# Gate, up and most of down products as 64-row couples on both halves of the array, with new load order and row grouping

## The chip, the cores and the metric

The kernel runs on one core of a Trainium2 chip. The metric is the device time of one execution in microseconds; "span" is the time from the first to the last instruction in the profile of one execution, some 2 us shorter than the time of the same execution.

Engines are named as in the profile: PE does the matrix products (PEld loads their weights), DVE the vector work, ACT the activations, POOL the third elementwise engine, SP issues transfers.

## The reference, cut to what matters

One transformer-like layer over 2048 tokens of width 448: layer norm, linear attention with 16 heads of 28 and a softmax feature map, a residual, layer norm, a gated feed-forward of width 1792, a residual.

```python
def _A_ref(x, wqkv, w_phi, wo):                    # x is already normalised
    q, k, v = split(x @ wqkv)                      # 448 x 1344
    pq = einsum("bhsd,hdf->bhsf", q, w_phi)
    pk = einsum("bhsd,hdf->bhsf", k, w_phi)
    phi_q = concatenate([softmax(pq), softmax(-pq)], axis=-1)
    phi_k = concatenate([softmax(pk), softmax(-pk)], axis=-1)
    kv = einsum("bhsf,bhsd->bhfd", phi_k, v)       # needs every token before any output
    z  = einsum("bhsf->bhf", phi_k)
    ...                                            # num / den, then @ wo

def _B_ref(x, w_gate, w_up, w_down):
    h = sigmoid(x @ w_gate) * (x @ w_up)           # 448 x 1792 each
    return h @ w_down                              # 1792 x 448

h  = x + _A_ref(layernorm(x), wqkv, w_phi, wo)
h2 = h + _B_ref(layernorm(h), w_gate, w_up, w_down)
```

Two facts matter. `kv` sums over all 16 tiles of 128 tokens, so no output of attention exists before the last tile's k features: that is the front of the kernel. And the contraction of gate and up, 448, is three and a half times 128: the array has 128 rows, so each gate and each up product has a remainder of 64 rows.

## The kernel before

The kernel is a graph of named operations. Each engine runs its operations in a fixed, hand-kept order (a list of names per engine), and semaphores are derived from reads and writes of tiles and PSUM banks. The feed-forward works in blocks of 128 of the 1792 columns, two blocks at a time ("a pair of blocks"). Before the change, a pair of blocks was three full gate products, three full up products, a couple of 64-row products for the remainders (gate on rows 0 to 63 of the array, up on rows 64 to 127, side by side), then the same with the couple first:

```python
def full(e, w, b, st, sp):
    for kt in range(3):
        p = e.matmul(bk(b)[:, 0:N], lhsT=w[:, kt, fs], rhs=hb[:, kt, ns],
                     start=(st and kt == 0), stop=(sp and kt == 2))
    return p

def pair(e, st):
    e.matmul(bk(bg)[:, 0:N], lhsT=wg_sb[0:64, 3, fs], rhs=hb[0:64, 3, ns], start=st, stop=not st)
    return e.matmul(bk(bu)[:, 0:N], lhsT=wu_sb[64:P, 3, fs], rhs=hb[64:P, 3, ns], start=st, stop=not st,
                    tile_position=(64, 0))
# even block: full(gate), full(up), pair    odd block: pair, full(gate) | full(up)
```

Down was 14 full products for each token tile. The loads of the front are made with k and v weights in separate transfers and one token tile's 128 rows spread one to a partition.

```python
x_t   = A_x[0].rearrange("(n p) d -> p n d", p=P)
out_t = out[0].rearrange("(n p) d -> p n d", p=P)
...
xload(0, 1, 100)
...
xload(1, 2, 97)
wload(1, "wk", 96.5)
wload(2, "wv", 96)
xload(2, 4, 95)
...
def warm(n):                       # products of zeros, to have the clock released early
    def f(e):
        for _ in range(n):
            p = e.matmul(bk(7)[:, 0:512], lhsT=zero[:, 0:P], rhs=zero[:], start=True, stop=True)
        return p
    return f
op("pe", "warm", warm(10), r=["zero"], w=[B(7)], dur=10 * 0.43, prio=100)
```

The k weights are transposed on PE, evicted, multiplied with `w_phi` (one product fewer per token later), evicted, and only then does the first k product run.

The softmax here doesn't subtract the row's maximum and nothing guards it: scores larger than these inputs give would overflow.

## Time and profile before

The time before is 224.34 us (median of four runs, 222.31 to 225.28). The span of the profiled execution, 222.8 us, falls into parts:

| part of the span | from, to (us) | length |
|---|---|---|
| start to first exp of k | 0, 12.80 | 12.80 |
| first exp of k to first gate product | 12.80, 71.14 | 58.34 |
| first gate product to start of the last product | 71.14, 219.30 | 148.16 |
| start of the last product to the end | 219.30, 222.8 | 3.5 |

PE's timeline: start, length of the group, engine, line, operation, tiles, shapes, count, and in brackets the idle time before it with what ended it.

```profile
1.49 3.62 PE L405 MATMUL psum<-zero 128*128 128x512 bf16 x10 [1.49 <-DVE zero L373]
6.14 0.62 PE L424 MATMUL psum<-ident,wqkv_sb 112*112 112x112 bf16 x8 [1.03 <-DMA wqkv_sb<-in_A_wqkv_dram]
...
9.69 0.92 PE L526 MATMUL psum<-wqkv_sb,xnT 112*128 112x448 bf16 x4
11.02 0.92 PE L526 MATMUL psum<-Wk,xnT 112*128 112x448 bf16 x4 [0.41 <-ACT Wk L445]
```

The k weights are in use at 6.14, released by their transfer, and the first k product starts at 11.02; the exponential of its result starts at 12.80. Four products in 0.92 us (their starts 0.19 apart) are at full speed.

The trace also holds records of the clock that was granted to PE. Here it was released at 4.13 us, during the warm-ups, and fell back to half speed from 24.61 to 28.03 us: the 7 in the row of the granted clock on the page.

In the second part ACT was the most loaded elementwise engine (windows view: length, then busy us and count of PE, PEld, DVE, ACT, POOL, granted clock, transfer share, GB/s):

```profile
12.80:71.14 58.34, 53.97 (x431) 33.80 (x428) 44.60 (x105) 52.52 (x107) 40.37 (x50) 0.97 0.68 145
```

### The profile page before, as it was taken

How to read it: one execution, taken by the hardware profiler on the slowest of the kernel's cores; microseconds unless marked ns; L12 is line 12 of the kernel's file. 1: busy time of each engine (PE TensorE's matmuls, PEld its weight loads, DVE VectorE, ACT ScalarE, POOL GpSimd, SP SyncE). 2: the span in 40 equal slices, each digit the busy share in tenths (PEclk: the TensorE clock that was granted, in tenths of full speed). 3: DMA queues.
4: the chain of work that ended last, by engine and by line, in shares of the span. 5: the costliest groups of instructions: out<-in, count | busy, mean ns of one | idle time of the engine just before them, and what ended most of it. 6: DMA issues, size and time to landing. Idle time of an engine off the chain costs nothing.

```text
span 222.8 us, 3721 instructions
## 1 busy us (share of the span) xinstructions
PE 210.5 (94%) x1392; PEld 111.4 (50%) x1402; DVE 137.9 (62%) x340; ACT 105.4 (47%) x219; POOL 67.4 (30%) x112
## 2 busy tenths in 40 slices
PE   6677899999998999999999999999999999999994
PEld 2444466666655666667634434433444344544351
DVE  3776977874978996799788858253531344232342
ACT  2797799987999554312343453233310322022210
POOL 5579789882344422222331410110000000000000
PEclk9999799999999999999999999999999999999999
DMA  6669899954004234204123131100010000010011
GB/s 156 153 170 147 210 167 272 218 164 128 0 0 74 47 71 57 42 24 91 27 49 71 30 66 47 24 14 9 24 41 0 22 24 21 0 41 21 3 41 41
DMA packets 31530, 15.61 MB, mean 70 GB/s; under 512 B 22936, under 2 KB 30616, under 8 KB 31512
## 3 DMA queue, kind: packets, MB, share of 16 engines
q1 hardware_dynamic: 31008, 15.34, 31.7%
q8 instruction: 11, 0.18, 0.3%
q10 hardware_dynamic: 504, 0.03, 0.2%
q14 instruction: 7, 0.06, 0.1%
HBM read 8.28 MB, written 1.84 MB: 45 GB/s over the span
## 4 chain that ended last, share of the span: by engine, by line
PE 80%; ACT 10%; DMA 6%; issue 1%; POOL 1%; DVE 0%; SPq 0%
PE psum L739 34%; PE psum L777 19%; PE psum L744 7%; PE psum L526 6%; PE psum L690 5%; PE psum L561 4%; PE psum L654 3%; ACT xn_pad L507 3%; DMA wqkv_sb<-in_A_wqkv_dram 2%; DMA xnT<-xn_pad 2%; PE psum L553 2%; DMA oT<-o_pad 2%; ACT hhT L537 1%; ACT hhT L536 1%; ACT WkT L429 1%
## 5 line engine op out<-in xcount | busy, mean ns | idle before, releaser
L764 ACT ACTIVATE sg_sb<-psum 128x512 bf16<-128x512 f32 (+1 forms) x70 | 35.7, 509 | 88.4 <-PE psum L745 80.8
L767 DVE TENSOR_TENSOR hhT<-psum,sg_sb 128x512 bf16<-128x512 f32 (+1 forms) x70 | 40.3, 581 | 45.2 <-ACT sg_sb L764 35.8
L739 PE MATMUL psum<-xnT,wu_sb 128*128 128x512 bf16 (+1 forms) x207 | 47.3, 336 | 0.3
L739 PE MATMUL psum<-xnT,wg_sb 128*128 128x512 bf16 (+1 forms) x203 | 46.7, 337 | 0.3 <-issue 0.2
L777 PE MATMUL psum<-wd_sb,hhT 128*128 128x448 bf16 x224 | 46.0, 352 | 0.1
L777 PEld LDWEIGHTS psum<-wd_sb,hhT 128*128 128x128 bf16 x224 | 21.8, 98 | 19.9 <-DVE hhT L767 0.2
L739 PEld LDWEIGHTS psum<-xnT,wu_sb 128*128 128x128 bf16 x210 | 20.5, 98 | 15.9
L739 PEld LDWEIGHTS psum<-xnT,wg_sb 128*128 128x128 bf16 x210 | 17.3, 97 | 22.1 <-issue 11.9
L545 POOL TENSOR_TENSOR phi<-hhT,rs 128x896 bf16<-128x896 bf16 x16 | 26.9, 1698 | 4.3 <-DVE rs L543 3.4
L676 POOL TENSOR_TENSOR o_pad<-c_sb,rden 128x448 bf16<-128x448 bf16 x16 | 14.9, 936 | 29.0 <-DVE rden L674 28.8
L541 DVE TENSOR_REDUCE ss<-hhT 128x32 f32<-128x896 bf16 x16 | 17.1, 1070 | 5.3 <-ACT hhT L537 5.2
L783 DVE TENSOR_TENSOR x_sb<-psum,x_sb 128x448 bf16<-128x448 f32 x16 | 9.9, 624 | 15.5 <-PE psum L777 15.0
L745 PE MATMUL psum<-xnT,wu_sb 64*128 64x512 bf16 (+1 forms) x70 | 18.1, 338 | 0.0
L744 PE MATMUL psum<-xnT,wg_sb 64*128 64x512 bf16 (+1 forms) x70 | 18.1, 338 | 0.0
L526 PE MATMUL psum<-Wk,xnT 112*128 112x448 bf16 x64 | 15.2, 363 | 2.8 <-DMA xnT<-xn_pad 2.3
L526 PE MATMUL psum<-wqkv_sb,xnT 112*128 112x448 bf16 x64 | 15.2, 368 | 1.2 <-ACT v L539 1.2
L561 PE MATMUL psum<-xnT,Wq 112*112 112x512 bf16 x64 | 16.2, 382 | 0.0
L690 PE MATMUL psum<-wo_sb,oT 112*128 112x448 bf16 x64 | 14.7, 352 | 0.3 <-DMA oT<-o_pad 0.3
L701 POOL TENSOR_SCALAR ve<-ssq 128x1 f32<-128x1 f32 x16 | 3.0, 190 | 39.0 <-ACT junk L698 38.8
L698 ACT ACTIVATE junk<-x_sb,nm 128x448 bf16<-128x448 bf16 x16 | 10.7, 671 | 7.7 <-DVE nm L696 7.6
L477 DVE BATCH_NORM_STATS2 st<-x_sb 128x6 f32<-128x448 bf16 x16 | 9.4, 612 | 5.5 <-DMA x_sb<-in_A_x_dram 5.5
L693 DVE SCALAR_TENSOR_TENSOR x_sb<-psum,x_sb 128x448 bf16<-128x448 f32 x16 | 9.9, 617 | 2.6 <-PE psum L690 2.3
(80 smaller groups left out, 249.7 us busy)
## 6 DMA issues: line engine op xcount, KB each, us to landing
out_dram<-x_sb SPq DMA_DIRECT2D x16, 112.0 KB, 1.7
wd_sb<-in_B_w_down_dram SPq DMA_DIRECT2D x7, 224.0 KB, 3.0
wu_sb<-in_B_w_up_dram SPq DMA_DIRECT2D x3, 448.0 KB, 4.5
wg_sb<-in_B_w_gate_dram SPq DMA_DIRECT2D x3, 448.0 KB, 4.0
wqkv_sb<-in_A_wqkv_dram SPq DMA_DIRECT2D x3, 392.0 KB, 4.8
x_sb<-in_A_x_dram SPq DMA_DIRECT2D x2, 448.0 KB, 4.5
x_sb<-in_A_x_dram SPq DMA_DIRECT2D x3, 224.0 KB, 4.3
wo_sb<-in_A_wo_dram SPq DMA_DIRECT2D x1, 392.0 KB, 3.7
```

The lines of the kernel that those rows point to most:

```text
L526: p = e.matmul(bk(bank)[:, 0:D], lhsT=xnT[t // 4][:GP, kt, TS(t)], rhs=wap(kt), start=(kt == 0), stop=(kt == KT - 1))
L541: op("dve", "ss%d" % t, lambda e: e.tensor_reduce(ss[:, s, :], ek[:, s, :, :].rearrange("p a (h d) -> p (a h) d", d=DH), AX.X, ALU.add), r ...
L545: op("pool", "phi%d" % t, lambda e: e.tensor_tensor(phi[:, sp, :, :].rearrange("p a (h d) -> p (a h) d", d=DH), ek[:, s, :, :].rearrange(" ...
L561: p = e.matmul(bk(b)[:GP, 0:512], lhsT=W2[1][:, kt, gg * GP:(gg + 1) * GP], rhs=xnT[c][:GP, kt, :], start=(kt == 0), stop=(kt == KT - 1))
L676: op("pool", "o%d" % t, lambda e: e.tensor_tensor(o_pad[:, s, :, 0:GP].rearrange("p g (h d) -> p g h d", h=4), c_sb[:, s, :, 0:DH].rearran ...
L690: p = e.matmul(bk(2)[:, 0:D], lhsT=oT[:GP, s, kt, :], rhs=wo_sb[:, kt, :], start=(kt == 0), stop=(kt == KT - 1))
L739: p = e.matmul(bk(b)[:, 0:N], lhsT=w[:, kt, fs], rhs=hb[:, kt, ns], start=(st and kt == 0), stop=(sp and kt == 2))
L744: e.matmul(bk(bg)[:, 0:N], lhsT=wg_sb[0:64, 3, fs], rhs=hb[0:64, 3, ns], start=st, stop=not st)
L745: return e.matmul(bk(bu)[:, 0:N], lhsT=wu_sb[64:P, 3, fs], rhs=hb[64:P, 3, ns], start=st, stop=not st, tile_position=(64, 0))
L764: op("act", "sig%d_%d" % (ci, ff), lambda e: e.activation(sg_sb[:, k, 0:N], bk(bg)[:, 0:N], ACT.Sigmoid), r=[B(bg), "sigtab"], w=[("sg", k ...
L767: op("dve", "hh%d_%d" % (ci, ff), lambda e: e.tensor_tensor(hhT[(t0 // 4) % NHH][:, ff, ns], bk(bu)[:, 0:N], sg_sb[:, k, 0:N], ALU.mult), ...
L777: p = e.matmul(bk(b)[:, 0:D], lhsT=hhT[c % NHH][:, ff, TS(t)], rhs=wd_sb[:, ff, :], start=(ff == 0), stop=(ff == FT - 1))
```

## The change

Its intent is to stop PE from switching between full products and 64-row products in the feed-forward: gate and up use 64-row couples throughout (low half of the array for one, high half for the other), the last three groups of token tiles do down the same way, and each pair of blocks or tiles swaps which bank each half writes to midway, so that each output gets all its rows. Beside that the change reorders the loads, loads k and v weights together in two halves of rows, gives each partition 16 consecutive token rows, moves thirteen operations (four evictions of k weights, five of v, three of transposed tokens and a normalisation) from ACT to DVE, against, on balance, two more evictions of q weights on ACT, and regenerates every engine's order. It also cuts the preparation of the k weights differently: each transposition needs only one of the two row halves, and each product with `w_phi` only one eviction in place of four. The core of the diff:

```diff
-    x_t = A_x[0].rearrange("(n p) d -> p n d", p=P)
-    out_t = out[0].rearrange("(n p) d -> p n d", p=P)
+    x_t = A_x[0].rearrange("(p n) d -> p n d", p=P)
+    out_t = out[0].rearrange("(p n) d -> p n d", p=P)
...
-        wload(1, "wk", 96.5)
-        wload(2, "wv", 96)
+        wload(0, 2, 1, 3, [("wkv", 0), ("wkv", 1)], "ld_kv0", 99, 220.0)
+        wload(2, 4, 1, 3, [("wkv", 2), ("wkv", 3)], "ld_kv1", 97, 220.0)
...   # order of SP: which transfers are asked for first
-        "x0 ld_wk x1 x2 ld_wv x4 x6 x8 ld_wq xT4 x12 ..."
+        "x0 x1 x2 x4 ld_kv0 ld_kv1 x8 x10 xT4 xT5 ld_q ..."
...
+        def both(e, lo, hi):
+            for a in range(max(len(lo), len(hi))):
+                for l, row in ((lo, 0), (hi, 64)):
+                    if a < len(l):
+                        o, w, r, st, sp = l[a]
+                        p = e.matmul(o, lhsT=w, rhs=r, start=st, stop=sp, tile_position=(row, 0))
+            return p
...
+            def f1(e):     # four couples: gate low, up high
+                return both(e, [(og, wg_sb[LO, kt, fs], hb[LO, kt, ns], kt == 0, False) for kt in range(4)],
+                            [(ou, wu_sb[HI, kt, fs], hb[HI, kt, ns], kt == 0, False) for kt in range(4)])
+            def f2(e):     # three couples, banks swapped
+                return both(e, [(ou, wu_sb[LO, kt, fs], hb[LO, kt, ns], False, kt == 2) for kt in range(3)],
+                            [(og, wg_sb[HI, kt, fs], hb[HI, kt, ns], False, kt == 2) for kt in range(3)])
...   # order of PE, one pair of blocks (even f1, odd f1, even f2, odd f2)
-        "gu0_0 gg0_1 uu0_1"
+        "ga0_0 ga0_1 gb0_0 gb0_1"
...   # a PE operation waits on PE itself when a bank changes halves
+            if o.eng == "pe":
+                return self.crosses(p, o)
...   # down of tiles 4 to 15, two tiles at a time, swapped midway
+                    def part(i, s):
+                        return [(bk(b[i])[:, 0:D], hb[s, ff, TS(t + i)], wd_sb[s, ff, :], ph == 0 and ff == 0,
+                                 ph == 1 and ff == FT - 1) for ff in range(a, a + n)]
+                    return both(e, part(i, LO), part(j, HI))
```

## The prediction

> **What bounds the kernel now.** I read the page first (busy shares, the row of slices, the granted clock), then the windows view over three stretches, then the PE waits of the first stretch, then the timeline of PE inside the late stage and of all engines in the tail.
>
> ```profile
> PE 210.5 (94%) x1392; PEld 111.4 (50%) x1402; DVE 137.9 (62%) x340; ACT 105.4 (47%) x219; POOL 67.4 (30%) x112
> ...
> PE   6677899999998999999999999999999999999994
> ...
> PEclk9999799999999999999999999999999999999999
> ```
>
> PE is loaded from end to end, but the first five slices (5.6 us each) are at 6 to 8 tenths, and the fifth ran at a lower clock. I split the span at the first v product (9.7), the first gate product (71.1) and the last stretch of down products (213).
>
> ```profile
> 9.70:71.10 61.40, 56.62 (x447) 35.14 (x446) 46.88 (x109) 55.58 (x113) 42.79 (x58) 0.97 0.66 142
> 71.10:213.00 141.90, 141.26 (x868) 69.61 (x876) 83.05 (x211) 45.62 (x100) 20.03 (x39) 1.00 0.16 35
> 213.00:222.80 9.80, 6.64 (x36) 3.23 (x33) 3.13 (x5) 0.00 (x0) 0.00 (x0) 0.99 0.14 47
> ```
>
> Columns: length, then busy us of PE, PEld, DVE, ACT, POOL. In the first stretch ACT (55.6 of 61.4) is as loaded as PE (56.6), so PE waits for it in part. In the second PE is never idle (141.3 of 141.9): only shorter PE work shortens it. PE's waits between 9 and 72 us:
>
> ```profile
> PE psum L526 <- DMA xnT<-xn_pad: 2.3, 1, 2.3
> PE psum L526 <- ACT v L539: 1.2, 1, 1.2
> ```
>
> "Busy" hides slower steps, so I looked at starts in the late stage. This is one pair of feed-forward blocks (gate and up of two blocks), between two runs of down products:
>
> ```profile
> 183.64 2.06 PE L777 MATMUL psum<-wd_sb,hhT 128*128 128x448 bf16 x10
> 185.53 0.81 PE L739 MATMUL psum<-xnT,wg_sb 128*128 128x512 bf16 x3
> 186.18 0.81 PE L739 MATMUL psum<-xnT,wu_sb 128*128 128x512 bf16 x3
> 186.92 0.39 PE L744 MATMUL psum<-xnT,wg_sb 64*128 64x512 bf16 x1
> 186.92 0.39 PE L745 MATMUL psum<-xnT,wu_sb 64*128 64x512 bf16 x1
> 187.15 0.38 PE L744 MATMUL psum<-xnT,wg_sb 64*128 64x512 bf16 x1
> 187.15 0.38 PE L745 MATMUL psum<-xnT,wu_sb 64*128 64x512 bf16 x1
> 187.46 0.82 PE L739 MATMUL psum<-xnT,wg_sb 128*128 128x512 bf16 x3
> 188.12 0.81 PE L739 MATMUL psum<-xnT,wu_sb 128*128 128x512 bf16 x3
> 188.76 1.49 PE L777 MATMUL psum<-wd_sb,hhT 128*128 128x448 bf16 x7
> ```
>
> Ten down products of 448 columns start over 1.89 us: 0.189 each, so 0.216 for 512 columns. The pair of blocks has 14 such slots (12 full products and two 64-row couples, each couple one slot, its halves starting together): 14 x 0.216 = 3.02. It takes 188.76 - 185.53 = 3.23. The missing 0.21 lies at the two borders between full and 64-row products: 186.18 to 186.92 is 0.74 where 0.65 is due, 187.15 to 187.46 is 0.31 where 0.22 is due. One change of mode costs 0.105 us. There are 35 such pairs (five groups of token tiles, seven pairs each) and so 70 changes, 7.3 us. The 256-column groups show the same borders (72.01 to 72.22 where 0.11 is due).
>
> **What the Trainium skill says.** (1) "TensorEngine Tiling (Array Packing)", Key Properties: changing the tiling mode drains the TensorE. The trace agrees and prices it at 0.105 us. (2) The same page, Gotcha 1: different row tiles cannot use one PSUM bank at once, software has to keep them apart. That is why the changed kernel swaps banks midway and makes PE wait on itself; this trace has no such wait. (3) "TensorE: Matmul & The Clock Gate", Part 3: products on different row groups run concurrently, starting about 4 ns apart. The trace agrees: both halves start at 186.92. (4) "DMA: Bandwidth & Descriptors", Specifications: line rate needs runs of 512 B or more. Token rows and weight rows come in runs of 896 B already, so longer runs should gain little; no run yet shows how much.
>
> **The change, part by part.**
>
> *Gate and up on both halves.* A block becomes four couples (gate low half, up high half), then three couples with the banks swapped: seven slots, 14 for a pair of blocks, as before. No column is saved. What goes are the borders. In the new PE order I counted the borders of full and 64-row work from the first gate product on: 18 islands of gate/up among full products (attention, wo and down of tiles 0 to 3), then one long 64-row run to the end, down products included. That is 37 changes in place of 70: 33 x 0.105 = **3.4 us less**, all on the bound stretch.
>
> *Down in couples (tiles 4 to 15).* 14 slots a tile as before, 0 us. Its use is that the last three groups never leave the mode. Each swap must wait for the other half's last product. From the order, something else lies between nearly everywhere; only the last two swaps of the kernel follow each other bare. A product shows 0.38 us where its slot is 0.22, so 0.16 of drain, plus semaphore and reload: I estimate 0.25 each, **0.5 us more**. The last two tiles now end together, so their two final additions (L783, two in 1.38) stand one after the other behind the last product:
>
> ```profile
> 218.93 1.38 DVE L783 TENSOR_TENSOR x_sb<-psum,x_sb 128x448 bf16<-128x448 f32 x2 [3.16 <-PE psum L777]
> ```
>
> Before, the first of the two ran beside the last products and only the second (0.69) stood behind them: **0.7 us more**.
>
> *Bank turnover.* Before, the even block of a pair is done seven slots before the odd one; now three. Its sigmoid and product start four slots later (0.43 us at 256 columns, 0.86 at 512). In the late groups the down products in between cover this. In the 256-column groups the filler is about 1 us and DVE is 80 to 88% busy: I allow **0.8 us more**.
>
> *Front.* Loads: x tiles 0 to 7 go first in longer runs, k and v weights come as two row halves holding k and v together. All 1.68 MB are asked for at once. Before, x tiles 4 to 7 were held back, their statistics waited 2.8 us, and the first transposing DMA was issued only at 15.13. I expect the weights complete at about 9.5 to 10 (wk landed at 6.1 before, wv by 9.6), so the first exp of k stays near 12.8 to 13.5; but by then eight token tiles are ready, which should remove most of the 1.2 and 2.3 us waits, and the half-speed spell after the second (four v products start at 25.39, the next four at 26.88: 0.37 each instead of 0.19, until 27.6, about 1.3 us). Work leaves ACT: five v evictions (0.55 each), two xnT evictions and one hn eviction (0.6 each), one normalisation (0.79), against two more weight evictions (1.15): ACT's 55.6 becomes about 51.6. With the old 5.8 us of ACT idleness the first gate product would come 4 us earlier, with half of it 7. PE gives the same limit: its idle and slow time in that stretch is about 8 us. I take **5.2 us less**; POOL's 16 phi products (1.70 each, 27 us after the first) and the DVE, which gets the moved work, keep it from more.
>
> Sum: -3.4 + 0.5 + 0.7 + 0.8 - 5.2 = -6.6 us, 224.55 to about 218.0.
>
> **Rivals.** *A couple costs more than a full slot.* 186.92 to 187.15 is 0.23, not 0.216. If that held in a long run, 70 x 7 + 12 x 14 = 658 slots would lose 0.01 each, 6.6 us, and the time would be about 224. Against it: the full products after a border also take 0.66 for three, not 0.65, so the first step after a drain seems long in either mode. I give it one chance in six. *The front is limited by DVE or POOL instead.* Then it gains 1 to 2 us and the result is about 221.5. For it: POOL was busy 8.0 to 9.5 of each 10 us there. Against: its idleness (3.4 us for rs) came from upstream. *The front gains all of its gaps* (7 to 8 us): about 215. *PE stalls on banks in every pair*, 0.3 us x 35: plus 10, seen at once as PE waits; the order of old shows none, and the new one interleaves down products for it, so unlikely.
>
> **Range and chances.** The drain part is a count times a measured cost (0.5 us of doubt). The front (2 to 8) and the couple's step carry the spread, some 3 us: 214.0 to 221.5. Two per cent is 220.06.
>
> **What would show it.** Right: couples 0.216 apart (0.109 at 256 columns), 37 borders, first gate product at 64 to 68, ACT less loaded and the clock at 9 throughout, PE gapless after it. Wrong: couples at 0.225, PE waits on itself or on ACT/DVE in the gate groups, first gate product still near 70, or weights landing after 11.

## The result and the profile after

| | median us | range | runs |
|---|---|---|---|
| before | 224.34 | 222.31 to 225.28 | 4 |
| after | 217.64 | 216.07 to 218.69 | 4 |

The ratio is 0.9708 (95% interval 0.9617 to 0.9798): faster. Ratios in this document are the mean time of one kernel's fast runs over the mean of the other's fast runs of the same rounds, so not quite the ratio of the medians quoted. Executions over 1.5% slower than the fastest of the same kernel are left out of the means. All outputs are right. The profiled execution of the changed kernel was the longest of its four (218.69 us, span 217.0); the others had spans of 214.4 to 216.2. Much of this spread has a cause that is found below.

The gain of this first job is on the large side. In the three later jobs the kernel before ran 82 times more, with medians of 222.96, 222.69 and 222.82 us. In 17 of its fast executions the mean granted clock is 0.992 or less, as in the one profiled, and their median is 224.01; that of the other 64 is 222.59. Against the changed kernel sent again (217.60) the gain is 5.4 us, ratio 0.9783 with an interval that includes 2%.

The page of the changed kernel:

```profile
PE 208.6 (96%) x1990; PEld 116.4 (54%) x1990; DVE 133.8 (62%) x353; ACT 99.4 (46%) x208; POOL 66.0 (30%) x110
...
PE   7599999999999999999999999999999999999992
...
PEclk9999999999999999999999999999999999999998
...
L745 PE MATMUL psum<-xnT,wg_sb 64*128 64x512 bf16 (+1 forms) x490 | 90.8, 334 | 0.0
L745 PE MATMUL psum<-xnT,wu_sb 64*128 64x512 bf16 (+1 forms) x490 | 90.5, 334 | 0.0
```

PE now stands at 9 in all slices but the first two and the last: what was weak after them is filled. There are 490 gate and 490 up products, all of 64 rows, with no idle time before them. ACT lost 6 us of work (105.4 to 99.4).

The same four parts, side by side, from the two profiled executions:

| part | before | after | difference |
|---|---|---|---|
| start to first exp of k | 12.80 | 16.77 | +3.97 |
| first exp to first gate product | 58.34 | 51.18 | -7.16 |
| first gate to start of last product | 148.16 | 145.00 | -3.16 |
| last product to end | 3.47 | 4.02 | +0.55 |
| span | 222.8 | 217.0 | -5.8 |

The difference of the second part holds the slow spell of the kernel before; that of the first part holds a slow start of the changed one, told below.

**Feed-forward.** PE's timeline of the changed kernel around a border between down and a pair of blocks:

```profile
197.16 0.54 PE L745 MATMUL psum<-wd_sb,hhT 64*128 64x448 bf16 x4
197.54 0.38 PE L745 MATMUL psum<-xnT,wg_sb 64*128 64x512 bf16 x1
197.54 0.38 PE L745 MATMUL psum<-xnT,wu_sb 64*128 64x512 bf16 x1
197.75 0.38 PE L745 MATMUL psum<-xnT,wg_sb 64*128 64x512 bf16 x1
197.76 0.38 PE L745 MATMUL psum<-xnT,wu_sb 64*128 64x512 bf16 x1
197.97 0.38 PE L745 MATMUL psum<-xnT,wg_sb 64*128 64x512 bf16 x1
...
203.21 0.38 PE L745 MATMUL psum<-xnT,wg_sb 64*128 64x512 bf16 x1
...
206.23 1.11 PE L745 MATMUL psum<-wd_sb,hhT 64*128 64x448 bf16 x10
```

The couples start 0.215 apart, the two halves within 0.01 of each other (0.02 in the first couples of 256 columns): a couple costs a slot and no more. A pair of blocks at 203.21 was followed by down at 206.23, so 14 slots took 3.02 us, exactly 14 x 0.216; before it was 3.23. There is no step at the change from down to gate any more, since both are 64-row work. And PE waits for nothing from the first gate product on (windows view, PE busy 137.05 of 137.05):

```profile
67.95:205.00 137.05, 137.05 (x1418) 72.56 (x1420) 76.51 (x210) 44.28 (x98) 20.11 (x39) 1.00 0.18 37
```

**Front.** The changed kernel's start, and then the view of PE's waits over the whole span (what waited, on whom, us in total, times, longest):

```profile
1.25 4.45 PE L418 MATMUL psum<-zero 128*128 128x512 bf16 x10 [1.25 <-DVE zero L385]
...
9.18 1.00 PE L438 MATMUL psum<-ident,wqkv_sb 112*112 112x112 bf16 x8 [1.39 <-DMA wqkv_sb<-in_A_wqkv_dram]
...
12.32 1.70 PE L534 MATMUL psum<-wqkv_sb,xnT 112*128 112x448 bf16 x4
...
15.82 1.68 PE L534 MATMUL psum<-Wk,xnT 112*128 112x448 bf16 x8
```

```profile
PE psum L438 <- DMA wqkv_sb<-in_A_wqkv_dram: 1.4, 1, 1.4
PE psum L418 <- DVE zero L385: 1.2, 1, 1.2
PE psum L465 <- DVE xn_pad L509: 1.0, 1, 1.0
PE psum L534 <- DMA xnT<-xn_pad: 0.5, 1, 0.5
PE psum L561 <- POOL phi L553: 0.3, 1, 0.3
```

Three things are to be seen. The weights are in use at 9.18 and not at 6.14. The first four v products take 1.70 us where four took 0.92 before: their starts are 0.37 apart, half speed, and so is everything on PE until about 14 us. The warm-up products tell the same: ten took 4.45 us, against 3.62 before, so the clock had not been released by their end. The first clock record of this trace starts at 13.97 us. The row of the granted clock on the page reads 9 before that all the same: time without a record is counted as full speed. And of the old waits of the first stretch (1.2 for ACT's eviction of v, 2.3 for a transposing transfer) only 0.5 is left. After the first exponential the front runs with hardly a gap:

```profile
16.77:67.95 51.18, 50.21 (x420) 32.47 (x419) 41.82 (x101) 46.11 (x96) 37.40 (x42) 1.00 0.57 150
```

PE is busy in 50.2 of 51.2 us here (54.0 of 58.3 before) and ACT's work fell from 52.5 to 46.1.

**Tail.** The last two final additions run one after the other behind the last product:

```profile
211.35 1.16 DVE L791 TENSOR_TENSOR x_sb<-psum,x_sb 128x448 bf16<-128x448 f32 x2 [2.51 <-PE psum L745]
...
213.34 1.16 DVE L791 TENSOR_TENSOR x_sb<-psum,x_sb 128x448 bf16<-128x448 f32 x2 [0.83 <-PE psum L745]
```

### The profile page after: what moved, and what is told of

It reads as the page before. It is cut to its first block, busy times and chain, and to the rows that moved or that the text cites.

```text
span 217.0 us, 4885 instructions
## 1 busy us (share of the span) xinstructions
PE 208.6 (96%) x1990; PEld 116.4 (54%) x1990; DVE 133.8 (62%) x353; ACT 99.4 (46%) x208; POOL 66.0 (30%) x110
## 4 chain that ended last, share of the span: by engine, by line
PE 80%; DMA 6%; DVE 6%; ACT 4%; POOL 2%; SPq 1%; issue 1%; DVEq 0%
PE psum L745 55%; PE psum L699 6%; PE psum L802 5%; PE psum L569 4%; PE psum L534 3%; DMA wqkv_sb<-in_A_wqkv_dram 3%; PE psum L661 3%; DMA xnT<-xn_pad 2%; PE psum L561 2%; POOL phi L553 2%; DMA x_sb<-in_A_x_dram 1%; ACT hhT L545 1%; ACT hhT L544 1%; DVE ss L549 1%; ACT xn_pad L508 1%; PE psum L438 1%
## 5 line engine op out<-in xcount | busy, mean ns | idle before, releaser
L745 PE MATMUL psum<-xnT,wg_sb 64*128 64x512 bf16 (+1 forms) x490 | 90.8, 334 | 0.0
L745 PE MATMUL psum<-xnT,wu_sb 64*128 64x512 bf16 (+1 forms) x490 | 90.5, 334 | 0.0
L786 DVE TENSOR_TENSOR hhT<-psum,sg_sb 128x512 bf16<-128x512 f32 (+1 forms) x70 | 39.1, 581 | 61.1 <-ACT sg_sb L783 61.0
L745 PEld LDWEIGHTS psum<-xnT,wg_sb 64*128 64x128 bf16 x490 | 44.6, 94 | 23.1 <-DVE hhT L786 2.0
L745 PEld LDWEIGHTS psum<-xnT,wu_sb 64*128 64x128 bf16 x490 | 44.6, 94 | 15.9
L745 PE MATMUL psum<-wd_sb,hhT 64*128 64x448 bf16 x336 | 34.9, 349 | 0.1
L745 PEld LDWEIGHTS psum<-wd_sb,hhT 64*128 64x128 bf16 x336 | 16.2, 94 | 17.0 <-PE psum L745 1.0
L802 PE MATMUL psum<-wd_sb,hhT 128*128 128x448 bf16 x56 | 13.0, 353 | 0.0
L661 PEld LDWEIGHTS psum<-kvz,eq 112*128 112x128 bf16 x128 | 8.4, 98 | 4.7 <-issue 0.8
L661 PE MATMUL psum<-kvz,eq 112*128 112x120 bf16 x128 | 10.9, 216 | 0.0
```

The source lines that it names most:

```text
L661: p = e.matmul(bk(bank)[:, gg * 4 * E:(gg + 1) * 4 * E], lhsT=eq[c][:, sg, gg, TS(t)], rhs=kvz[:, sg, gg, :], start=True, stop=True)
L745: p = e.matmul(o, lhsT=w, rhs=r, start=st, stop=sp, tile_position=(row, 0))
L786: op("dve", "hh%d_%d" % (ci, ff), lambda e: e.tensor_tensor(hhT[(t0 // 4) % NHH][:, ff, ns], bk(bu)[:, 0:N], sg_sb[:, k, 0:N], ALU.mult), ...
L802: p = e.matmul(bk(b)[:, 0:D], lhsT=hhT[c % NHH][:, ff, TS(t)], rhs=wd_sb[:, ff, :], start=(ff == 0), stop=(ff == FT - 1))
```

## The experiments

My theory after reading the traces had four parts. (1) The whole gain of the feed-forward is the borders between full and 64-row products; couples as such cost and save nothing. (2) The front lost time because the weights come later and the clock was still low, and gained it back because more tokens are ready early and ACT has less to do. (3) The longer rows do nothing. (4) The two bare bank swaps and the doubled final addition at the end are small. The rivals: couples save or cost by themselves; late weights delay the front one for one; the longer rows make the loads faster; what matters is the order alone. Of the eleven kernels below the first is the changed kernel itself and the others are edits of it, sent in three jobs. Columns of times are median, range, and ratio to the kernel before in the same job.

| kernel | median | range, runs | ratio [95%] | profiled span | weights in use | first exp | first gate | gate to last product |
|---|---|---|---|---|---|---|---|---|
| after_again | 217.60 | 217.08 to 220.02, 6 | 0.9783 [0.9738, 0.9829] | 214.3 | 8.44 | 14.64 | 65.30 | 145.00 |
| all_full | 221.76 | 219.90 to 223.06, 22 | 0.9947 [0.9923, 0.9970] | 221.3 | 8.80 | 17.24 | 68.53 | 148.78 |
| dn_full | 220.68 | 219.96 to 221.97, 7 | 0.9893 [0.9852, 0.9934] | 220.2 | 8.95 | 16.99 | 68.22 | 148.02 |
| warm_long | 216.76 | 216.64 to 217.23, 6 | 0.9728 [0.9698, 0.9759] | 215.5 | 9.24 | 15.29 | 66.49 | 145.00 |
| weights_first | 223.18 | 221.98 to 225.36, 22 | 1.0026 [1.0006, 1.0047] | 222.0 | 7.34 | 14.87 | 72.64 | 145.33 |
| old_rows | 218.46 | 216.47 to 219.70, 6 | 0.9792 [0.9745, 0.9840] | 217.0 | 8.90 | 16.73 | 67.95 | 145.01 |
| tail_fix | 218.42 | 216.64 to 219.34, 6 | 0.9791 [0.9749, 0.9833] | 217.5 | 8.83 | 16.97 | 68.61 | 144.53 |
| best1 | 223.08 | 221.82 to 225.91, 22 | 0.9993 [0.9969, 1.0017] | 220.9 | 7.12 | 13.64 | 71.99 | 144.53 |
| v_on_act | 220.62 | 219.17 to 221.71, 6 | 0.9885 [0.9845, 0.9926] | 219.7 | 8.34 | 16.34 | 70.69 | 145.00 |
| kv_split | 217.80 | 216.67 to 218.27, 6 | 0.9756 [0.9718, 0.9794] | 215.0 | 8.46 | 15.37 | 65.94 | 145.00 |
| mid_order | 218.78 | 218.13 to 219.25, 6 | 0.9801 [0.9768, 0.9833] | 216.3 | 7.79 | 15.31 | 67.32 | 145.00 |

The clock records say when each profiled execution ran at half speed in its front. In after, weights_first and v_on_act it was up to about 14 us. In all_full, dn_full, old_rows, tail_fix and kv_split the clock was released at 4.0 to 5.0 us, during the warm-ups, and taken back at 7.4 to 8.5, for 6.8 us (3.4 in kv_split). In best1 it was half from 16.29 to 23.11. In after_again, warm_long and mid_order it stayed full from 6.2 to 6.8 us on. A page shows a clock that was taken back, here all_full's in the second and third slice and best1's in the fourth:

```profile
PEclk9769999999999999999999999999999999999998
```

```profile
PEclk9995999999999999999999999999999999999999
```

### after_again: the changed kernel unchanged

No edit. It gives the jobs their own yardstick and shows how far two executions of the same kernel differ.

> The changed kernel itself, unedited, as the reference point for the runs beside it. The four runs so far lie between 216.07 and 218.69 us, and all ten warm-up products of the profiled one ran at half speed. Theory (the spread is the moment at which the PE clock is released): again a spread of 2 us or so, median 217 to 218; a profile in which the warm-up reaches full speed has its first exp of k at 14.5 or earlier instead of 16.8. Rival (spread is other noise): the first exp stays within 0.3 us of 16.8 whatever the warm-up shows.

Measured: 217.60 us, ratio 0.9783. Its profiled span is 214.3, 2.7 below that of the first profile, and the feed-forward is the same to the hundredth (145.00). So the whole difference lies in the front. PE's timeline there:

```profile
1.24 4.45 PE L418 MATMUL psum<-zero 128*128 128x512 bf16 x10 [1.24 <-DVE zero L385]
...
8.43 0.62 PE L438 MATMUL psum<-ident,wqkv_sb 112*112 112x112 bf16 x8 [1.35 <-DMA wqkv_sb<-in_A_wqkv_dram]
...
10.33 0.92 PE L534 MATMUL psum<-wqkv_sb,xnT 112*128 112x448 bf16 x4
```

The weights landed 0.74 earlier, and the v products are at full speed: the clock was released between the warm-ups and 8.4 us here, and only near 14 us in the first profile (by the clock records at 6.75 and 13.97). From weights in use to first exponential it is 6.20 us here and 7.59 there. So the slow clock costs 1.4 us in an execution where it occurs, and the landing varies by some 0.7 us.

### dn_full: down of tiles 4 to 15 as full products again

```diff
-                    return both(e, part(i, LO), part(j, HI))
+                    for ff in range(a, a + n):
+                        p = e.matmul(bk(b[ph])[:, 0:D], lhsT=hb[:, ff, TS(t + ph)], rhs=wd_sb[:, ff, :],
+                                     start=(ff == 0), stop=(ff == FT - 1))
```

Gate and up stay in couples. The borders come back, one on each side of every run of down products, and the two bare bank swaps at the end go, since full products need none.

> Only the down products of tiles 4 to 15 go back to full products; gate and up stay in couples with swapped banks. In this order there are again 70 borders. Theory (borders are the whole gain, couples of 64 rows are free): the same stretch as with everything full, 148.0 us, total about 220.5. Rival (the gate and up couples have a value of their own): the stretch lies nearer 145 than 148. A second rival (a couple costs 0.01 us more than a slot): it lies above 148 by up to 5 us, since the 490 gate and up couples remain.

Measured: gate to last product 148.02, against 145.00, and 220.68 us. PE's timeline:

```profile
203.79 0.38 PE L745 MATMUL psum<-xnT,wg_sb 64*128 64x512 bf16 x1
204.10 2.82 PE L817 MATMUL psum<-wd_sb,hhT 128*128 128x448 bf16 x14
206.85 0.39 PE L745 MATMUL psum<-xnT,wg_sb 64*128 64x512 bf16 x1
...
207.08 0.38 PE L745 MATMUL psum<-xnT,wg_sb 64*128 64x512 bf16 x1
```

From the last couple to down it is 0.31 where a slot is 0.216; 14 down products of 0.189 end at 206.75 and the couple starts at 206.85; the slot after the border is 0.23. So each border costs 0.095 to 0.10 and a little more in the slot that follows, as the prediction's 0.105 had it. The trace of this kernel has 69 borders from the first gate product on and that of the changed kernel 36. The stretch is 3.02 us longer although it is without the two swaps, worth 0.47 (see tail_fix), so the 33 borders cost 3.5, 0.106 each. All 490 couples of gate and up are still there and save nothing. Part (1) of the theory holds, and the rival that couples as such cost or save something falls.

### all_full: gate and up as before too

```diff
-                return both(e, [(og, wg_sb[LO, kt, fs], hb[LO, kt, ns], kt == 0, False) for kt in range(4)],
-                            [(ou, wu_sb[HI, kt, fs], hb[HI, kt, ns], kt == 0, False) for kt in range(4)])
+                if j == 0:
+                    full(e, og, wg_sb, True, False)
+                    return couple(e, False)
+                couple(e, True)
+                return full(e, og, wg_sb, False, True)
...
-                return both(e, [(ou, wu_sb[LO, kt, fs], hb[LO, kt, ns], False, kt == 2) for kt in range(3)],
-                            [(og, wg_sb[HI, kt, fs], hb[HI, kt, ns], False, kt == 2) for kt in range(3)])
+                return full(e, ou, wu_sb, False, True)
```

together with the edit of dn_full; order, loads and evictions stay those of the changed kernel.

> Front, orders and banks of the changed kernel, but gate, up and down as full products with one couple each, as before: 70 borders of mode instead of 37 and no swap waits. Theory (a border costs 0.105 us): first gate product to last product 145.0 plus 33 x 0.105 = 3.5 minus two bare swaps of 0.22, so 148.0 us, and a total of about 220.5. Rival (the couples themselves save or cost something, or the gain came from the front alone): the stretch stays at 145 and the total within 1 us of the changed kernel; or it rises by clearly more than 3.5.

Measured: gate to last product 148.78, time 221.76. The borders now stand at the middle couple of each pair of blocks instead of at the edges of down, 70 of them:

```profile
202.92 0.38 PE L745 MATMUL psum<-xnT,wu_sb 64*128 64x512 bf16 x1
203.22 0.82 PE L761 MATMUL psum<-xnT,wg_sb 128*128 128x512 bf16 x3
...
205.18 1.11 PE L826 MATMUL psum<-wd_sb,hhT 128*128 128x448 bf16 x5
```

From couple to full it is 0.30 again, and from the last gate and up product to down no step. That is as many borders as dn_full has and nearly the same length of the feed-forward; of the 0.76 us between them 0.52 is one single gap before a gate product that follows an attention product. This is the kernel before in its products and the kernel after in everything else: it keeps 0.5% of the 2.2% that the changed kernel gained in this job, so the 64-row products are worth about 1.6%, or 3.7 us between the means of this job (4.2 between the medians). The feed-forward of the profiles has 3.8 of it (148.78 against 145.00). What is left to the loads, the evictions and the orders is the 0.5%, 1.2 us. That is less than the 3.2 us by which the two first profiles differ at the first gate product: it also pays for the single gap and for the longer tail, most executions of the kernel before have no slow spell, and in the profiled execution of all_full the clock was half from 8.4 to 15.2 us (first exponential at 17.24).

### warm_long: more warm-up products

```diff
-        op("pe", "warm", warm(10), r=["zero"], w=[B(7)], dur=10 * 0.43, prio=100)
+        op("pe", "warm", warm(13), r=["zero"], w=[B(7)], dur=13 * 0.43, prio=100)
+        op("pe", "warmb", warm(8, 2), r=["zero"], w=[B(2)], dur=8 * 0.43, prio=100)
...   # order of PE
-        "warm xT0 xT1 wT0_0 ..."
+        "warm xT0 xT1 warmb wT0_0 ..."
```

PE's idle time before the weights is filled with products of zeros, so that the clock is released before the chain begins.

> The changed kernel with 13 instead of 10 warm-up products and 8 more after the first two token transposes, into a bank that is still free, so that PE is busy until the k and v weights land at about 9.2 us. Theory (the products from 9.2 to 14 us ran at half clock because the clock was never released or fell back): v and k products start 0.19 apart from the beginning, first exp of k at 14 to 14.8 instead of 16.8, first gate product at 65.5 to 67 instead of 68, total about 1.5 to 2 us less than the changed kernel and with less spread. Rival (the front is bound by what follows on ACT, DVE and POOL, or the weights): the first exp comes earlier but the first gate product stays within 0.5 us of 68.

Measured: 216.76 us with a range of only 0.59 us over six runs, where after_again in the same job had 2.94. PE's timeline:

```profile
7.50 1.89 PE L418 MATMUL psum<-zero 128*128 128x512 bf16 x8
9.23 0.58 PE L439 MATMUL psum<-ident,wqkv_sb 112*112 112x112 bf16 x8
...
11.09 0.92 PE L535 MATMUL psum<-wqkv_sb,xnT 112*128 112x448 bf16 x4
```

The weights are in use as late as in the first profile (9.24 against 9.18), but the chain to the first exponential takes 6.05 us and not 7.59, and both the first gate product (66.49 against 67.95) and the span (215.5 against 217.0) come 1.5 us earlier. So a late first exponential costs the end one for one when nothing else changes. The clock is shown as the cause of that part, and of most of the spread: the spans of these six executions lie between 214.9 and 215.5, those of after_again between 214.3 and 217.4, and none of the six has a mean granted clock below 0.995, where after_again goes down to 0.981. Whether the three warm-ups more or the eight in the gap did it was not tried apart. Its median is the lowest of all kernels run, 0.84 us below the changed one in the same job (the two sets of six overlap by one run). Single executions of the changed kernel were as fast or faster (216.07).

### weights_first: the k and v weights before the third token tile

```diff
-        "x0 x1 x2 x4 ld_kv0 ld_kv1 x8 ..."
+        "x0 x1 ld_kv0 ld_kv1 x2 x4 x8 ..."
```

with the first operations of PE, ACT and DVE put in an order by hand that goes with it.

> The changed kernel with the k and v weights asked for after token tiles 0 and 1 instead of after tiles 0 to 7, and the first orders of PE, ACT and DVE adapted so that nothing waits for tiles 2 and 3 before the first k and v products. In five profiles of the changed front the first gate product came 50.7 to 51.3 us after the first exp of k, whenever that was. Theory (the late weights delay the whole front one for one): weights landed by 7 us, first exp at 12 to 13.5 instead of 14.6 to 17.2, first gate product at 63.5 to 65, total 214 to 215.5. Rival (the early token tiles are what makes the 51 us possible): the exp comes earlier, but the distance to the first gate product grows by as much, total 217 to 218.

Measured: the weights are in use at 7.34 and the first exponential at 14.87, 1.9 us earlier than in the first profile, but the first gate product is at 72.64, 4.7 later, and the time is 223.18, no better than the kernel before. The waits of PE up to 80 us, and the window from the first exponential to the first gate product:

```profile
PE psum L534 <- DVE xnT L426: 2.2, 1, 2.2
PE psum L534 <- DMA xnT<-xn_pad: 1.9, 2, 1.6
```

```profile
14.87:72.64 57.77, 52.31 (x433) 33.38 (x432) 48.35 (x118) 48.21 (x99) 40.04 (x50) 1.00 0.60 145
```

PE stands for the third and fourth token tile (an eviction on DVE, 2.2) and for a transposing transfer (1.6), and the stretch takes 57.8 us as it did before the change (58.3). So earlier weights did not bring an earlier end here. But it is not shown that the loads are to blame, for the tokens' data did not come late. This is the trace from 9 to 14 us (windows view), and then DVE's timeline:

```profile
9.00:14.00 5.00, 5.00 (x33) 3.41 (x33) 2.83 (x9) 2.48 (x5) 1.39 (x5) 1.00 0.00 0
```

```profile
10.16 0.77 DVE L426 COPY WkT<-psum 112x448 bf16<-112x448 bf16 x2 [1.45 <-PE psum L438]
10.85 1.14 DVE L479 BATCH_NORM_STATS2 st<-x_sb 128x6 f32<-128x448 bf16 x2
...
15.04 1.14 DVE L479 BATCH_NORM_STATS2 st<-x_sb 128x6 f32<-128x448 bf16 x2
...
17.77 0.72 DVE L426 COPY xnT<-psum 112x512 bf16<-112x512 bf16 x2
```

Nothing is transferred from 9 to 14 us: all that had been asked for, tiles 0 to 7 among it, had landed. Yet DVE takes the statistics of tiles 2 and 3 only at 10.85 (at 5.19 in the changed kernel), since the order made by hand puts the weights' evictions first, and DVE waits for PE there. And the eviction for which PE waits starts at 17.77, although PE was done with transposing at 16.03, because that order has the statistics of tiles 4 to 7 before it, from 15.04 on. So some 1.7 of that wait's 2.2 us come from the order made by hand. How much of the 6.6 us between 51.2 and 57.8 does, and what the order of loads costs or wins by itself, stays open.

### old_rows: one token row to a partition again

```diff
-    x_t = A_x[0].rearrange("(p n) d -> p n d", p=P)
-    out_t = out[0].rearrange("(p n) d -> p n d", p=P)
+    x_t = A_x[0].rearrange("(n p) d -> p n d", p=P)
+    out_t = out[0].rearrange("(n p) d -> p n d", p=P)
```

> The changed kernel with the rows of a token tile taken one after the other as before, 896 bytes a run, in loads and stores. Theory (runs of 896 bytes are long enough, the regrouping is nearly free of effect): the x load of four tiles lands up to 0.7 us later and the k and v weights behind it up to 0.7 us later, first gate product at most 0.7 us later, total within 1 us of the changed kernel. Rival (regrouping is a main part of the front's gain): first exp 2 us later or more, total about 219.5.

Measured: 218.46 us; span 217.0, first gate product 67.95, gate to last product 145.01: the same as the first profile of the changed kernel in each. The transfer of four token tiles takes 5.1 us from issue to landing instead of 4.7, but nothing later in the front shows it. The clock was half for about as much of the chain from the weights to the first exponential (5.3 us, 4.8 in the first profile), so the two may be compared. The longer rows are worth nothing that these runs resolve.

### tail_fix: one step between the last two swaps

```diff
-        "... dn12_8 dn12_10 dp14_12 dp12_8 dp12_10 dn12_12 dp12_12"
+        "... dn12_8 dn12_10 dn12_12 dp14_12 dp12_8 dp12_10 dp12_12"
```

> The changed kernel with the last low-and-high down couples of tiles 12 and 13 moved ahead of the swap, so that the two swaps that stood bare at the very end lie behind other work. Theory (each bare swap costs PE 0.225 us): first gate product to last product 144.55 instead of 145.00 us; total 0.45 less, which the clock's scatter may hide. Rival (PE then waits for the sigmoid and product of the last block): the stretch stays at 145.0.

Measured: gate to last product 144.53, 0.47 less; the two gaps of 0.225 us that the changed kernel's starts show at 212.0 and 212.6 are gone. But now four final additions queue on DVE behind the last products:

```profile
212.39 2.29 DVE L791 TENSOR_TENSOR x_sb<-psum,x_sb 128x448 bf16<-128x448 f32 x4 [2.89 <-PE psum L745]
```

and the time from the last product to the end grows from 4.02 to 4.36. The net 0.13 us cannot be seen in the time (218.42). A bare swap is priced at 0.225 us, and it was in part hidden by the additions.

### best1: weights first, twelve warm-ups and tail_fix together

```diff
-        "x0 x1 x2 x4 ld_kv0 ld_kv1 x8 ..."
+        "x0 x1 ld_kv0 ld_kv1 x2 x4 x8 ..."
-        op("pe", "warm", warm(10), r=["zero"], w=[B(7)], dur=10 * 0.43, prio=100)
+        op("pe", "warm", warm(12), r=["zero"], w=[B(7)], dur=12 * 0.43, prio=100)
```

with the orders of weights_first and tail_fix.

> Weights first, 12 instead of 10 warm-up products, and the tail reordered, together. Theory: the three add up: first exp at 11.5 to 13, first gate product at 63 to 64.5, then 144.55 and a tail of 4.0, total 213 to 214.5 with the fixed 1.7 us between span and time. Rival as for the weights alone: 216.5 to 217.5.

Measured: 223.08 us, ratio 0.9993. It was meant as the best version and is not. Its first exponential is the earliest of all changed kernels (13.64, the clock was released), and the first gate product is at 71.99 all the same: 58.3 us between them, as in the kernel before. It cannot confirm weights_first with a released clock, since here the clock fell back to half speed from 16.29 to 23.11 us, within that stretch, and the orders made by hand are the same. The clock is not all of it, though: PE's wait for the same eviction on DVE, 2.6 us here, begins before that spell, and the four executions with a mean granted clock of 1.000, which had no such spell, took 221.82 to 223.17 us, much like the others.

### v_on_act: the five v evictions back on ACT

```diff
   # order of ACT
-        "... ek0 ek1 xn6 ek2 v1_2 ek3 ek4 ... ek8 ek9 xn12 ... ek10 ek11 xn15 ..."
+        "... ek0 ek1 v1_3 xn6 ek2 v1_2 ek3 v1_5 ek4 ... ek8 ek9 v1_9 xn12 ... ek10 ek11 v1_10 v1_11 xn15 ..."
```

and the five names taken out of DVE's order.

> The changed kernel with the five v evictions that had gone to DVE (tiles 3, 5, 9, 10, 11) back on ACT, each in the place that the order of PE gives it. Theory (ACT binds from the first exp of k to the first gate product): the distance between the two grows from 51.2 us by up to 5 x 0.55 = 2.7, to 52.5 to 54, total 1.5 to 2.5 us over the changed kernel. Rival (PE or POOL binds there, and the shorter distance comes from the early tokens alone): the distance stays at 51 to 51.7.

Measured: 220.62 us, 2.8 us above kv_split in the same job, and the first gate product at 70.69, 2.7 later than in the first profile although the first exponential came 0.43 earlier:

```profile
16.34:70.69 54.35, 50.88 (x421) 32.52 (x420) 39.94 (x94) 48.39 (x101) 37.48 (x42) 1.00 0.56 141
```

ACT does 2.3 us more in this stretch (48.39 against 46.11), and the stretch is 3.2 us longer. DVE's 1.9 us less buy nothing. PE's waits there, where the changed kernel has only 0.5 for the transposing transfer:

```profile
PE psum L534 <- DMA xnT<-xn_pad: 1.6, 2, 1.0
...
PE psum L534 <- ACT hhT L545: 0.6, 1, 0.6
PE psum L534 <- ACT v L426: 0.6, 1, 0.6
```

In neither profile does the clock fall back in this stretch. So with these evictions on ACT it is ACT, not DVE, that holds up the front, and in this order they cost at least the time that they take there; without them PE is left nearly gapless. Where on ACT they stand was chosen by hand, so another place might cost less.

### kv_split: k weights and v weights in separate loads again

```diff
-        wload(0, 2, 1, 3, [("wkv", 0), ("wkv", 1)], "ld_kv0", 99, 220.0)
+        wload(0, 4, 1, 2, ["wk"], "ld_wk", 99, 220.0)
...
-        wload(2, 4, 1, 3, [("wkv", 2), ("wkv", 3)], "ld_kv1", 97, 220.0)
+        wload(0, 4, 2, 3, ["wv"], "ld_wv", 97, 220.0)
```

> The changed kernel with the weights of k and v loaded as before, all of k and then all of v, in runs of 896 bytes instead of 1792. Theory (loading them as one matters little): first transposition of the weights at most 0.7 us later, the second pair without its wait, first exp within 0.7 us of the changed kernel at the same clock, total within 1 us. Rival (runs of 1792 bytes or the start on half of the rows are worth more): first exp 1.5 us later or more.

Measured: 217.80 us; weights in use at 8.46, first gate product 65.94, as in after_again (8.44, 65.30) with a clock that fell back to half speed from 8.45 to 11.86 us. Loading k and v as one is worth nothing that these runs resolve.

### mid_order: weights one token load earlier, with the longer warm-up

```diff
-        "x0 x1 x2 x4 ld_kv0 ld_kv1 x8 ..."
+        "x0 x1 x2 ld_kv0 ld_kv1 x4 x8 ..."
```

with 13 and 3 warm-ups (warm_long has 13 and 8) and a few first operations of ACT and DVE moved by hand.

> Between the changed kernel and the one with weights first: tiles 0 to 3, then the k and v weights, then tiles 4 to 7; early ACT and DVE orders adapted; 13 and 3 warm-up products. Theory (what the weights-first order lost was tiles 2 to 7, and the transposing DMAs behind them): weights in use at 7.5 to 8, first exp at 13 to 13.8, distance to the first gate product between 51.2 and 57.8, most likely 53, so first gate product near 66.5 and a total like that of the longer warm-up, 216 to 217.5. Rival (only tiles 0 to 3 matter): distance 51.2, first gate product at 64.5 to 65, total 214 to 215.

Measured: 218.78 us, slower than warm_long and no gain over the changed kernel. The weights are in use at 7.79, 1.45 earlier than in warm_long, but the first exponential is at 15.31 as there. PE's waits in this stretch add up to 1.5 us (0.7 for the eviction of the k weights on DVE, 0.5 and 0.2 for normalised tokens), which is what the earlier landing had won; and the stretch after it is 0.8 us longer. My hand-made order is to blame for the first; whether that order or the later fourth load makes the second is not shown.

## Why the prediction was right, and where its steps were not

The total was right: 6.6 us less predicted, 6.7 less in the median, 5.8 in the two profiled spans. The verdict (faster by over 2%) was too, in the first job. There is luck in both: the same kernel sent again gained 5.4 us, a verdict of unclear; and of the terms the front was taken for too much (5.2, measured 3.2) and the bank turnover for a loss that did not come (0.8), which cancel in part. Step by step:

**Borders, 3.4 us less: right.** The traces have 36 borders in place of 70 (predicted 37), each about 0.095 us over a slot (35 of the 36 from 0.094 to 0.096) plus about 0.01 in the next one. dn_full puts 33 of them back, is rid of the two bare swaps and loses 3.02 us, so the borders cost 3.5. The Trainium skill ("TensorEngine Tiling (Array Packing)", Key Properties) says that a change of mode drains the engine; these runs agree, and give the price.

**Rival "a couple costs more than a full slot": fell.** In long runs a couple is 0.215 to 0.216 us, and the halves start within 0.01 us. The long step that had spoken for it was the first slot after a drain.

**Two bare swaps, 0.5 us more: right.** Two gaps of 0.225 us, gone in tail_fix.

**Bank turnover, 0.8 us more: wrong, it is 0.** PE has no wait from the first gate product to 205 us. I had worked out how much later the even block's sigmoid starts, and then charged it to PE without a wait in the trace to charge it to; what PE does next in the 256-column groups (down, attention, wo) is longer than that.

**Tail, 0.7 us more: nearly right**, 0.55.

**Front, 5.2 us less: right in kind, 3.2 measured, and its working failed at one step.** The step is "I expect the weights complete at about 9.5 to 10 (wk landed at 6.1 before, wv by 9.6), so the first exp of k stays near 12.8 to 13.5". The landing was right: the first half is in use at 9.18. The "so" was not. The exponential does not hang on the last landing but on the k weights, and a chain of 6.66 us lies between: at 6.14 in the kernel before, and 9.18 + 6.66 = 15.8 was to be expected. Measured was 16.77 in the first profile, which is 3.97 later: 3.04 from the landing, 1.4 from the clock that was not yet released, and about 0.5 back because the chain itself is shorter at full speed (6.2). The missing term was made good in part by the other: I had counted on the waits of 1.2, 2.3 and the slow spell of 1.3 us, together with ACT's lighter load, for 5 to 6 us; the stretch from the first exponential to the first gate product became 7.2 shorter. Of these, v_on_act shows that five evictions on ACT are worth up to 3.2. About 1.4 is the slow spell of the profiled kernel before, an estimate from the medians of its executions with and without a clock so low (224.01 and 222.59). The rest, some 2.6, is not assigned. That early tokens are worth several us is not shown: weights_first and best1, meant to show it, lose at least part of their time by orders made by hand, with the tokens' data lying ready. How much belongs to the new orders as such stays open, since the eviction moves and the orders cannot be undone apart from each other without making yet another order by hand. The prediction's sum for ACT is slightly off as well: its own terms give 51.4 and not 51.6, and it leaves out the four evictions of k weights that also went to DVE.

**"The clock at 9 throughout" was no test.** The row of the granted clock does read 9, also over the products before 14 us that start 0.37 apart, because the trace has no clock record before the first release. The starts tell a late release, the row does not; a clock that was released and taken back the row does tell (6 to 8 in the second and third slice of five pages).

**Parts without effect.** Longer rows (old_rows) and the joined loads (kv_split) change nothing that is resolved, as the prediction said from runs of 896 bytes being long already.

The spread of the changed kernel, 216.1 to 220.0 over its two sets of runs, is for the most part the clock at the beginning: warm_long has 216.6 to 217.2. The profiles bear this out: from weights in use to the first exponential it takes 6.1 to 6.2 us where none of it was at half speed (warm_long, after_again), 6.9 where 3.4 us were (kv_split), 7.6 where 4.8 were (after), and 7.8 to 8.5 where 5.3 to 6.4 were (old_rows, v_on_act, dn_full, tail_fix, all_full). For the executions without a profile it is inference.

## What to carry to other kernels

Count the borders between full products and products on part of the array: at about 0.1 us each they are hidden in a PE that looks 94% busy, and uniform couples remove them at no cost. When a load is put back, carry the whole chain that hangs on its landing along, not just the landing; and then look at which engine sets the pace behind it, since a few evictions less on that engine can win back what the delay loses (five of them up to 3.2 us here). An order made by hand that goes with an edit is a second edit: before the load is blamed, see in the trace whether its data already lay ready. A clock that must be released at the start is worth having in hand: fill PE's idle time before the first useful work and read the result from the distance of starts. And a profile is one execution: compare its clock with that of the others before its parts are taken for the kernel's.

## What the Trainium skill lacked or had wrong

- "TensorEngine Tiling (Array Packing)", Key Properties: that a change of tiling mode drains the engine is stated without a price. These runs: about 0.095 us per change, either way, and some 0.01 us in the next slot; 33 changes cost 3.5 us.
- The same page, Gotcha 1, states that row tiles cannot share a bank at once, but not what handing a bank from one half to the other costs when nothing lies between: 0.225 us over a slot, twice in the changed kernel; with other products in between, nothing.
- "TensorE: Matmul & The Clock Gate", Part 1: it puts the release of the clock at around 4 us of sustained activity, give or take 0.5 us, though it says elsewhere in that part that it varies from run to run. Here the spread was wider: with ten warm-up products the release came 2.65 to 3.80 us after the first of them in six profiles, 5.5 us after it in one (after_again), and 12.5 to 12.7 in three (after, v_on_act, weights_first), although in weights_first PE stood idle for no more than 0.5 us at a time until then. In five of the six it was taken back at 7.4 to 8.5 us, with no idle time of PE between over 1.7 us. Thirteen and eight warm-ups without the gap made the time steady (a range of 0.6 us in place of 2.9).
- None has how the time before the first clock record of a trace is to be read. The profile's views count it as full speed: they give 1.00 for 9.00 to 14.30 us of the first profile, where starts are 0.37 apart (0.19 is full speed) and the first record is at 13.97.
